# Two attention blocks on one core: units halved by queries, eight-head projections, wider DMA transposes, and maxima as bf16 trees

## The chip, the cores and the metric

The kernel runs on one core of one Trainium2 chip. The metric is the device time of one execution in microseconds (us). A core has TensorE (PE in the profile; PEld is its weight load), VectorE (DVE), ScalarE (ACT), GpSimd (POOL) and SyncE (SP), which here only issues transfers. Each engine works through its own list of instructions in order and waits on semaphores for the others.

## The reference

Two independent blocks, A and B, each over 2048 rows of 512 features, with 32 heads of 16 dimensions. Their outputs stand side by side in the result.

```
# A: softmax attention
q, k, v = split((x @ wqkv).reshape(B, S, 3, H, Dh))
p = softmax(einsum("bhqd,bhkd->bhqk", q, k) * Dh ** -0.5, axis=-1)
a = einsum("bhqk,bhkd->bhqd", p, v).reshape(B, S, D) @ wo
# B: linear attention with a learned feature map
pq, pk = q @ w_phi[h], k @ w_phi[h]
phi(p) = concatenate([softmax(p), softmax(-p)])
kv = phi_k.T @ v;  z = phi_k.sum(rows)
b = (phi_q @ kv / (phi_q @ z + 1e-6)).reshape(B, S, D) @ wo
```

A does nearly all of the work: 32 heads with 2048 x 2048 scores each. B's feature map needs, for each row and head, the maximum and the minimum of 16 values.

## The kernel before

**Units.** A is cut into 32 units: 8 groups `g` of four heads times 4 chunks `c` of 512 queries. The four heads of a group lie on four row groups of TensorE (32 rows each: 16 dimensions, two rows for the maximum, the rest unused), so that matmuls on different row groups run side by side.

**Pass 1** finds the maximum of each query's scores. A unit has 32 steps: a step (`emit_m1`, L889) multiplies 128 queries of two heads with 512 keys into two PSUM banks, and VectorE takes the maximum over the keys (`emit_r1`, L903: 128 partitions x 2 x 512). Two pairs of banks alternate. At the end of a segment (below) `emit_mchain` combines the maxima of the four key chunks (L913), splits their negative into two bf16 parts on POOL (L918 to L921), turns them with a DMA transpose (L923) and writes them into rows of `QT` with two transfers (L926).

**Pass 2** multiplies 128 keys with 512 queries of one head (`block_go`, L954). The maximum is subtracted by the matmul itself, through the extra rows. ScalarE takes the exponential into a ring of 15 buffers (L960), three PSUM banks alternating. A unit has 64 such blocks. After each four, `pv_go` (L1008) multiplies them with the values, the four heads on four column groups, and adds up in bank 7; a column of ones gives the sum. `emit_xev`, `emit_rec` and `emit_mul` (L1137) divide by it. Pass 2 of a segment may start `LAGX` = 8 step slots after its last maximum.

**Segments.** A unit is one segment, but for the first and the last unit, which are cut into two: heads 0 and 1, then heads 2 and 3. Where a batch has only two heads, L1000 fills the other column groups with zero matmuls.

**Background jobs.** Projections of A (`proj`: four matmuls and a copy for each group of four heads and each chunk, L457 with L433, L465 or L469; for the values L445), the output projection (`oproj_job`, L820), and all of B run as jobs in pieces between the steps. B's feature map (`fm`): projection (L583), copy `pB` (L433), maximum and minimum on VectorE (`red`, L593 and L596), subtraction on POOL (L603, L605), exponential (L611), sums and division on POOL; then L697, L746 and L793 for the two products and the output. The last unit's output projection starts with `emit_acc` (L1152), seven matmuls in a lump for each of four row tiles, and ends in `emit_last`.

**The order.** A loop at the end of the kernel writes TensorE's whole list in advance. It goes by a plan of times (`_Clock`: a step 1.131, a matmul of 512 columns 0.215, an exponential 0.477) and puts in a job piece, a PV batch, a block or a step as they fit. Where the plan sees TensorE idle too long, it puts in fill matmuls on zeros, which hold the clock up: on four column groups (`go_fill`, L1101, 256 columns) or on a free row group beside a block (`row_fill`, L1086, 512 columns). At run time nothing is reordered; each instruction waits for its semaphores.

**The head.** x of A comes in 16 DMA transposes of 512 x 128 on SP (L301, four for each chunk of 512 rows), the weights in three loads of 512 columns (L289). VectorE clears the padded weight buffers (L304, L305) and spreads the heads' columns into them (`pad_copy`, L312). SP loads `B_w_phi` with 32 transfers (L517), and transposes B's weights (L529) and x (L533).

Of the kernel before, what the change touches and what calls it, by code (L numbers as in the profile page):

```python
# [6 lines left out]
ALU = mybir.AluOpType  # L7
# [141 lines left out]
def bass_concat_heads__softmax_full_mha__linear_kernel_hedgehog__prompt_kernel(  # L149
# [12 lines left out]
    SPLIT = {0, NU - 1}  # L162
# [20 lines left out]
    for u in range(NU):  # L183
        segs += [(u, (0, 1)), (u, (2, 3))] if u in SPLIT else [(u, (0, 1, 2, 3))]
# [3 lines left out]
    for v, (u, rows) in enumerate(segs):  # L188
        steps = [(v, rows[i] // 2, qt, kc) for kc in range(NKC) for qt in range(4) for i in range(0, len(rows), 2)]
        if u == 0 and v == 1:  # L190
            order[4:4] = steps[0:4]
            steps = steps[4:]
        order += steps
    steps_of = [[q for q, o in enumerate(order) if o[0] == v] for v in range(NV)]
    seg_end = [qs[-1] + 1 for qs in steps_of]
    of_b = [v for v in range(NV) for _ in range(NKT * len(segs[v][1]))]
    seg_b = [of_b.index(v) for v in range(NV)]
    LAG = seg_end[0] + LAGX

    with contextlib.ExitStack() as es:  # L200
# [33 lines left out]
        WQp = sb("WQp", [128, 4, NG, 128], BF)  # L234
        WKp = sb("WKp", [128, 4, NG, 128], BF)
# [15 lines left out]
        pB = sb("pB", [128, 2, 512], F32)  # L251
# [3 lines left out]
        mB = sb("mB", [128, 2, 2, 32], F32)  # L255
# [32 lines left out]
        def load_w(queue, i):  # L288
            t_wa[i] = P.dma(queue, dsem("wa%d" % i), lambda e: e.dma_start(  # L289
                wA[:, :, i * 512:(i + 1) * 512], wa_v[:, :, i * 512:(i + 1) * 512]))  # L290

        load_w("act", 0)
        load_w("act", 1)
        t_xa = {}
        for c in range(NQC):
            d = "xa%d" % c
            dsem(d)
            if c == 1:
                load_w("sp", 2)
            for ct in range(4):  # L300
                t_xa[c] = P.dma("sp", d, lambda e, ct=ct, c=c: e.dma_start_transpose(  # L301
                    xAT[:, ct, c * 512:(c + 1) * 512], A_x[0][c * 512:(c + 1) * 512, ct * 128:(ct + 1) * 128]))

        t_wq0 = P.op("dve", lambda e: e.memset(wqf.bitcast(U32), 0))  # L304
        t_wk0 = P.op("dve", lambda e: e.memset(wkf.bitcast(U32), 0))  # L305
        t_bias = P.op("dve", lambda e: e.tensor_reduce(
            bias_k[:, :], ident[:].rearrange("p (r x) -> p r x", x=32)[:, :, 16:18], AX.XY, ALU.add), [t_ident])

        def pad_copy(dst, col0, dep0):
            src = wA[:, :, col0:col0 + 512].rearrange("p ct (gr d) -> p ct gr d", d=16)  # L310
            dv = dst[:].rearrange("p ct g (r x) -> p ct (g r) x", x=32)[:, :, :, 0:16]
            return P.op("dve", lambda e: e.tensor_copy(dv, src), [t_wa[col0 // 512], dep0])  # L312
# [8 lines left out]
        t_yd1 = P.op("pool", lambda e: e.memset(Yd[:], 1.0))  # L321
        t_vb1 = P.op("pool", lambda e: e.memset(vB[:], 1.0))
# [37 lines left out]
        def add_job(slot, pieces, fin, by=None, when=None):  # L360
            by = slot + BY if by is None else by
            njobs[0] += 1
            jobs.append((by, slot, njobs[0], pieces, fin, when))

        def next_job(tau):

            return min((j for j in jobs if j[1] <= tau and (j[5] is None or j[5]())), default=None)

        ck = _Clock(12.0)
# [6 lines left out]

        def bg_at(tau):

            if running:
                left = running[0][0]  # L380
                return (ck.full("full", running[0][4]), left[0][0]) if left else None
            j = next_job(tau)
            if j is None or not ring_free:
                return None
            return ck.full("full", min(ring_free)[0]), j[3][0][0]

        def bg_go(tau):
            if not running:
                j = next_job(tau)
                jobs.remove(j)  # L390
                free, bank = ring_take()
                running.append([list(j[3]), j[4], bank, bank_reader.get(bank), free, None, j[0]])
            r = running[0]
# [9 lines left out]
        def bg_read(tau, by):  # L403


            if running and not running[0][0] and running[0][4] <= by:
                r = running.pop()
# [32 lines left out]
        last_proj = {}  # L440

        def proj(kind, a, c):
            if kind == "v":
# [3 lines left out]
                    start=(ct == 0), stop=(ct == 3)), [t_xa[kt // 4], t_wa[2]])  # L447
# [8 lines left out]
            wpad = WQp if kind == "q" else WKp  # L456
            pieces = mm_pieces(lambda e, b, ct: e.matmul(  # L457
                PS[:, b, :], wpad[:, ct, g, :], xAT[:, ct, c * 512:(c + 1) * 512],
                start=(ct == 0), stop=(ct == 3)), [t_xa[c], t_wqp if kind == "q" else t_wkp])

            def fin(b, tok, tau):
                last_proj[kind] = tok
                sl = slice(c * 512, (c + 1) * 512)
                if kind == "q" and g == 0 and c == 0:
                    t = P.op("dve", lambda e: e.tensor_copy(QT[:, g, sl], PS[:, b, :]), [tok])  # L465
                elif kind == "q":
# [4 lines left out]
                (qt_ready if kind == "q" else kt_ready)[(g, c)] = t  # L471
                return t
# [6 lines left out]
        XA = (9.0, 15.0, 19.5, 24.5)  # L479
        need = [(8, "k", 0, 1), (12, "k", 0, 2), (16, "k", 0, 3)]  # L480
# [6 lines left out]
        for g in range(2, NG):  # L487
            for t in group(g):
                add_job(at, *proj(*t), by=at + 10)
                at += 4  # L490
# [835 lines left out]
```

## Time and profile before

| | before |
|---|---|
| time of the runs | 1285.52 us median of 3 (1283.88 to 1287.56) |
| profiled execution: time / span | 1283.74 us / 1282.0 us |
| granted TensorE clock | 0.998 |
| PE, DVE, ACT, POOL busy, share of the span | 95%, 95%, 92%, 47% |
| maxima of pass 1 (L903) | 1024, 1170.2 us |
| exponentials of pass 2 (L960) | 2048, 1062.0 us |
| copies of B's maps: maxima and minima (L593, L596) | 32 each, 21.6 us each |
| maxima chains (L913) | 34, 6.9 us |
| DMA: share of 16 engines, main queue | 13.6% |

Busy times are unions: instructions of one engine that overlap count once. The span runs from the first to the last instruction of the core; the time of a run has some 2 us more. A row of the groups reads: line, engine, operation, result<-operands with shapes, count, then busy us and mean ns of one, then the idle time of the engine just before these instructions and what ended most of it.

### The profile page before, as it was taken

To read this page: it belongs to the slowest core of one execution; us is meant where nothing else is said; L and a number is where in the kernel's file an instruction comes from. 1 tells how busy PE (TensorE), PEld (TensorE's weight loads), DVE (VectorE), ACT (ScalarE), POOL (GpSimd) and SP (SyncE) were. 2 spreads that over 40 slices of the span, in tenths; PEclk is the share of its full clock that TensorE was granted. 3 is DMA by queue.
4 is the path that set the end of the run, shared out by engine and by line. 5 is a ranking of instruction groups with operands and counts; after the bars stand their busy time and mean duration, and the time that the engine had idled before them with its cause. 6 is when DMAs were issued, how large, how long until landed. Compare 5 with 4: busy or idle time off the path is not lost.

```text
span 1282.0 us, 28798 instructions
## 1 busy us (share of the span) xinstructions
PE 1219.7 (95%) x12059; PEld 408.0 (32%) x12059; DVE 1214.9 (95%) x1132; ACT 1180.3 (92%) x2321; POOL 600.8 (47%) x620
## 2 busy tenths in 40 slices
PE   8999999999999999999999999999999999999998
PEld 2223333333332233333333333333333233333333
DVE  8999999999999999999999999999999999999920
ACT  3789999999998999999999899999999999999986
POOL 2000102544655565546646346556555554646640
PEclk9999999999999999999999999999999999999999
DMA  6212200000001000000001110112211202121110
GB/s 132 60 16 40 35 7 4 7 7 7 7 6 19 6 8 7 7 6 3 7 7 7 23 24 11 31 19 20 32 19 27 36 15 32 23 24 19 29 20 21
DMA packets 75209, 26.69 MB, mean 21 GB/s; under 512 B 65928, under 2 KB 73096, under 8 KB 75080
## 3 DMA queue, kind: packets, MB, share of 16 engines
q1 hardware_dynamic: 73736, 23.56, 13.6%
q8 instruction: 94, 1.54, 0.5%
q10 hardware_dynamic: 1344, 1.31, 0.3%
q14 instruction: 35, 0.29, 0.1%
HBM read 3.16 MB, written 4.19 MB: 6 GB/s over the span
## 4 chain that ended last, share of the span: by engine, by line
ACT 51%; PE 27%; DVE 21%; issue 1%; DMA 0%; SPq 0%; ACTq 0%
ACT pT L960 45%; DVE part L903 20%; PE PS L954 7%; PE PS L889 4%; PE PS L457 3%; PE PS L1101 3%; PE PS L1008 2%; PE PS L583 2%; ACT eB L611 1%; PE PS L445 1%; PE PS L793 1%; PE PS L684 1%; ACT X L433 1%; ACT pB L433 1%; PE PS L1152 1%
## 5 line engine op out<-in xcount | busy, mean ns | idle before, releaser
L903 DVE TENSOR_REDUCE part<-PS 128x2 f32<-128x1024 f32 x1024 | 1170.2, 1215 | 5.7 <-PE PS L889 2.2
L960 ACT ACTIVATE pT<-PS 128x512 bf16<-128x512 f32 x2048 | 1062.0, 637 | 67.2 <-PE PS L954 27.0
L954 PE MATMUL PS<-QT,KT 32*128 32x512 bf16 x2048 | 657.1, 384 | 18.1 <-ACT pT L960 2.6
L1086 PE MATMUL PS<-zmv,ones_t 32*128 32x512 bf16 x1745 | 581.9, 382 | 0.3 <-ACT X L433 0.2
L889 PE MATMUL PS<-KT,QT 32*128 32x512 bf16 x2048 | 447.3, 383 | 14.1 <-DVE part L903 10.6
L954 PEld LDWEIGHTS PS<-QT,KT 32*128 32x128 bf16 x2048 | 176.9, 91 | 400.0 <-ACT pT L960 243.7
L1008 PE MATMUL PS<-pT,VP 128*17 128x512 bf16 x2048 | 210.7, 384 | 9.9 <-ACT pT L960 0.8
L918 POOL TENSOR_SCALAR stage<-mrow 128x16 bf16<-128x16 f32 (+1 forms) x34 | 8.8, 259 | 332.9 <-DVE mrow L913 332.9
L1101 PE MATMUL PS<-zmv,ones_t 128*17 128x256 bf16 x3028 | 146.7, 276 | 1.5
L1086 PEld LDWEIGHTS PS<-zmv,ones_t 32*128 32x128 bf16 x1745 | 143.3, 91 | 1.7 <-ACT X L433 1.1
L889 PEld LDWEIGHTS PS<-KT,QT 32*128 32x128 bf16 x2048 | 97.5, 91 | 122.3 <-DVE part L903 90.3
L1122 POOL TENSOR_TENSOR lr<-lr,neg 128x16 f32<-128x16 f32 x31 | 90.1, 2906 | 80.6 <-DMA lr<-X 80.5
L1008 PEld LDWEIGHTS PS<-pT,VP 128*17 128x17 bf16 x2048 | 51.4, 87 | 130.2 <-issue 69.3
L769 POOL TENSOR_TENSOR den_t<-den_t,neg 128x32 f32<-128x32 f32 x16 | 87.1, 5445 | 1.3
L641 POOL TENSOR_TENSOR wB<-wB,neg 128x32 f32<-128x32 f32 x16 | 87.0, 5440 | 0.8
L1101 PEld LDWEIGHTS PS<-zmv,ones_t 128*17 128x17 bf16 x3028 | 60.5, 90 | 80.4 <-issue 70.2
L1137 POOL TENSOR_TENSOR QT<-X,Yd 128x256 bf16<-128x256 f32 x62 | 43.8, 728 | 55.7 <-DMA Yd<-Yd 55.7
L618 POOL TENSOR_TENSOR sB<-eB 128x512 f32<-128x512 bf16 x32 | 36.9, 1154 | 67.3 <-ACT eB L611 67.3
L661 POOL TENSOR_TENSOR wA<-eB,rB 128x512 bf16<-128x512 bf16 x64 | 67.0, 1069 | 1.6
L603 POOL TENSOR_TENSOR uB<-pB,mB 128x512 f32<-128x512 f32 x32 | 33.9, 1060 | 52.0 <-DVE mB L593 52.0
L1176 DVE TENSOR_TENSOR QT<-PS,Yd 128x256 bf16<-128x256 f32 x2 | 0.8, 419 | 52.4 <-ACT Yd L1171 52.4
L583 PE MATMUL PS<-WKp,xBT 128*128 128x512 bf16 x128 | 38.0, 384 | 1.7 <-ACT pT L960 0.2
(85 smaller groups left out, 671.5 us busy)
## 6 DMA issues: line engine op xcount, KB each, us to landing
Yd<-Yd SPq DMA_DIRECT2D x124, 32.0 KB, 3.2
out_dram<-xAT SPq DMA_DIRECT2D x16, 128.0 KB, 1.8
out_dram<-OA SPq DMA_DIRECT2D x12, 128.0 KB, 1.7
wA<-in_A_wqkv_dram ACTq DMA_DIRECT2D x2, 512.0 KB, 5.1
QT<-mcols SPq DMA_DIRECT2D x60, 4.0 KB
mcols<-stage SPq DMA_TRANSPOSE x34, 2.3
wA<-in_A_wqkv_dram SPq DMA_DIRECT2D x1, 512.0 KB, 4.3
WOp<-in_A_wo_dram SPq DMA_DIRECT2D x4, 128.0 KB, 4.2
```

The source lines that it names most:

```text
L583: add_job(slot, mm_pieces(lambda e, b, ct: e.matmul(PS[:, b, :], xBT[:, ct, st * 128:(st + 1) * 128], Wf[:, x, ct, :], start=(ct == 0), st ...
L641: t = P.op("pool", lambda e: e.tensor_tensor(wB[:, n % 4, :], wB[:, n % 4, :], neg1[:, 0:1].broadcast_to([128, 32]), ALU.pow), [cx["r"], t ...
L661: t = P.op("pool", lambda e, a=a: e.tensor_tensor(f4[:, :, a, :], e4[:, :, a, :], r2[:, :, 1 - a].unsqueeze(2).broadcast_to([128, H, 16]), ...
L769: cx["rd"] = P.op("pool", lambda e: e.tensor_tensor(den_t[:, :], den_t[:, :], neg1[:, 0:1].broadcast_to([128, 32]), ALU.pow), [t, t_neg])
L889: tok = P.op("pe", lambda e, r=r, bank=2 * (q1 % 2) + i: e.matmul(PS[:, bank, :], QT[32 * r:32 * r + 32, g, q0:q0 + 128], KT[32 * r:32 * r ...
L903: r1[q1] = P.op("dve", lambda e: e.tensor_reduce(part[:, u % 2, 2 * pr:2 * pr + 2, qt, kc], PS[:, b:b + 2, :], AX.X, ALU.max), deps)
L954: m2_t[B] = P.op("pe", lambda e: e.matmul(PS[:, bank, :], KT[32 * r:32 * r + 32, g, kt * 128:(kt + 1) * 128], QT[32 * r:32 * r + 32, g, c ...
L960: exp_t[B] = P.op("act", lambda e: e.activation(pT[:, slot, :], PS[:, bank, :], ACT.Exp, scale=0.25), [m2_t[B], slot_reader.get(slot)])
L1008: tok = P.op("pe", lambda e, B=B, r=r: e.matmul(PVB[32 * r:32 * r + 17, :], VP[:, kt, 4 * g + r, :], pT[:, B % RING, :], start=(kt == 0), ...
L1086: fill_tok[0] = P.op("pe", lambda e: e.matmul(PS[:, 7, :], ones_t[32 * r:32 * r + 32, :], zmv[32 * r:32 * r + 32, :], start=False, stop=Fa ...
L1101: P.op("pe", lambda e, cq=cq: e.matmul(PS[32 * cq:32 * cq + 17, bank, 0:256], ones_t[:, 0:17], zmv[:, 0:256], start=(bank != 7), stop=(ban ...
L1122: rec = P.op("pool", lambda e: e.tensor_tensor(lr[:, ub, :], lr[:, ub, :], neg1[:, 0:1].broadcast_to([128, 16]), ALU.pow), [lr_t[u], t_neg])
```

## The change

It has five parts.

1. **Segments are runs of queries, not pairs of heads.** Every unit is cut into two segments of 256 queries, with all four heads; the first unit into 128, 128 and 256, the last into 256, 128 and 128. A block of pass 2 still fills a bank of 512 columns: with 256 queries it holds two key tiles (`per` = 2, two matmuls of 256 columns on the same row group), with 128 queries four. PV batches follow, eight matmuls of 256 columns for four of 512. The zero fills L1000 go. The key matrix has its heads' dimensions in even rows and ones in odd rows, so the maximum's two parts go to rows 1 and 17 of each group and one transfer writes them.
2. **Eight-head projections.** For groups 2 to 7, a projection of q or k makes 128 columns, eight heads at once. ScalarE copies it to a staging tile, and two transfers of 64 partitions x 512 spread it to the rows of the two groups. POOL presets these rows. Groups 0 and 1 keep the padded way.
3. **Wider DMA transposes.** x of A and B: one transpose of 512 x 512 for each chunk, instead of four; B's weights in 4 instead of 8; `B_w_phi` in 8 transfers instead of 32. A's weights come in five loads, the columns of the first two groups first.
4. **B's maxima and minima** of two maps at a time, as two trees of pairwise bf16 maxima and minima, interleaved; `pB` and `mB` become bf16.
5. **The plan.** It starts at 8.5 instead of 12.0, knows when projections are ready (`m1_from`), can have two jobs in hand, and runs `emit_acc`'s matmuls as a job in pieces.

```diff
-    SPLIT = {0, NU - 1}
+    SPLIT = {**{u: (2, 2) for u in range(NU)}, 0: (1, 1, 2), NU - 1: (2, 1, 1)}
@@ order
-    for v, (u, rows) in enumerate(segs):
-        steps = [(v, rows[i] // 2, qt, kc) for kc in range(NKC) for qt in range(4) for i in range(0, len(rows), 2)]
+    for v, (u, q0, nq) in enumerate(segs):
+        steps = [(v, pr, qt, kc) for kc in range(NKC) for qt in range(q0, q0 + nq) for pr in range(2)]
         if u == 0 and v == 1:
-            order[4:4] = steps[0:4]
-            steps = steps[4:]
+            order[2:2] = steps[0:2]
+            steps = steps[2:]
@@ head
-            if c == 1:
-                load_w("sp", 2)
-            for ct in range(4):
-                t_xa[c] = P.dma("sp", d, lambda e, ct=ct, c=c: e.dma_start_transpose(
-                    xAT[:, ct, c * 512:(c + 1) * 512], A_x[0][c * 512:(c + 1) * 512, ct * 128:(ct + 1) * 128]))
+            t_xa[c] = P.dma("sp", dsem("xa%d" % c), lambda e, c=c: e.dma_start_transpose(
+                xAT[:, :, c * 512:(c + 1) * 512], A_x[0][c * 512:(c + 1) * 512, :]))
+            if c == 2:
+                load_w("sp", 1024, 1536)
+        load_w("sp", 128, 512)
+        load_w("sp", 640, 1024)
@@ eight-head projections
+        def rows_of(g):
+            t_kt1[g] = P.op("pool", lambda e: e.memset(KT[:, g:g + 2, :].bitcast(U32), 0x3F803F80))
+            t_qt0[g] = P.op("pool", lambda e: e.memset(QT[:, g:g + 2, :].bitcast(U32), 0))
...
+                if g >= 2:
+                    i = n_oct[0] % 2
+                    n_oct[0] += 1
+                    t = aevac(oct_t[:, i, :], PS[:, b, :], [tok, oct_d.get(i)])
+                    dst, dep = (QT, t_qt0) if kind == "q" else (KT, t_kt1)
+                    for gg in range(2):
+                        oct_d[i] = P.dma("sp", d_oct[i], lambda e, gg=gg: e.dma_start(
+                            dst[0:128:2, g + gg, sl], oct_t[64 * gg:64 * gg + 64, i, :]), [t, dep[g]])
...
-        for g in range(2, NG):
+        for g in range(2, NG, 2):
             for t in group(g):
                 add_job(at, *proj(*t), by=at + 10)
-                at += 4
+                at += 6
@@ red
-                cx["mx"] = P.op("dve", lambda e: e.tensor_reduce(mB[:, i, 0, :], p3, AX.X, ALU.max),
-                                [cx["p"]] + use(("m", i)))
-                ck.extra += 1.19
-                cx["mn"] = P.op("dve", lambda e: e.tensor_reduce(mB[:, i, 1, :], p3, AX.X, ALU.min), [cx["p"]])
+                if i == 0:
+                    first_map[:] = [cx, sub]
+                    return
+                ops = (ALU.max, ALU.min)
+                src = pB[:].rearrange("p a (h f) -> p (a h) f", f=16)
+                t3 = [uB[:, 0, 256 * k:256 * k + 256].bitcast(BF).rearrange("p (h f) -> p h f", f=8) for k in range(2)]
+                ts = [P.op("dve", lambda e, k=k: e.tensor_tensor(t3[k], src[:, :, 0:8], src[:, :, 8:16], ops[k]),
+                           [cx["p"], first_map[0]["p"]] + use(("u", 0))) for k in range(2)]
+                for w in (4, 2):
+                    ts = [P.op("dve", lambda e, k=k, w=w: e.tensor_tensor(
+                        t3[k][:, :, 0:w], t3[k][:, :, 0:w], t3[k][:, :, w:2 * w], ops[k]), [ts[k]]) for k in range(2)]
+                ts = [P.op("dve", lambda e, k=k: e.tensor_tensor(
+                    mB[:, :, k, :].unsqueeze(3), t3[k][:, :, 0:1].rearrange("p (a h) f -> p a h f", a=2),
+                    t3[k][:, :, 1:2].rearrange("p (a h) f -> p a h f", a=2), ops[k]),
+                    [ts[k]] + use(("m", 0)) + use(("m", 1))) for k in range(2)]
+                ck.extra += 1.85
@@ emit_mchain
-            for hl in range(2):
-                mr_t[v] = P.dma("sp", d_mr[vb], lambda e, hl=hl: e.dma_start(
-                    QT[32 * rows[0] + 16 + hl:32 * rows[-1] + 32:32, g, c * 512:(c + 1) * 512],
-                    mcols[n * hl:n * hl + n, vb, :]), [mt_t[v]])
+            mr_t[v] = P.dma("sp", d_mr[vb], lambda e: e.dma_start(
+                QT[1:128:16, g, c * 512 + qs * 128:c * 512 + (qs + nq) * 128], mcols[0:2 * n, vb, :]), [mt_t[v]])
@@ block_go
-            m2_t[B] = P.op("pe", lambda e: e.matmul(
-                PS[:, bank, :], KT[32 * r:32 * r + 32, g, kt * 128:(kt + 1) * 128],
-                QT[32 * r:32 * r + 32, g, c * 512:(c + 1) * 512],
-                start=True, stop=True, tile_position=(32 * r, 0)),
-                [bank_reader.get(bank), mr_t[v], kt_ready[(g, kt // 4)]])
+            lo, w = c * 512 + qs * 128, nq * 128
+            for j in range(per):
+                m2_t[B] = P.op("pe", lambda e, j=j: e.matmul(
+                    PS[:, bank, j * w:j * w + w], KT[32 * r:32 * r + 32, g, (kt + j) * 128:(kt + j + 1) * 128],
+                    QT[32 * r:32 * r + 32, g, lo:lo + w],
+                    start=True, stop=True, tile_position=(32 * r, 0)),
+                    [bank_reader.get(bank), mr_t[v], kt_ready[(g, kt // 4)]] if j == 0 else [],
+                    signal=(j == per - 1))
@@ pv_go
+            for j in range(per):
+                for B in Bs:
+                    r = blk[B]
+                    tok = P.op("pe", lambda e, B=B, r=r, j=j: e.matmul(
+                        PVB[32 * r:32 * r + 17, lo:lo + w], VP[:, kt + j, 4 * g + r, :],
+                        pT[:, B % RING, j * w:j * w + w],
+                        start=(first and j == 0), stop=(kt + j == NKT - 1), tile_position=(0, 32 * r),
+                        skip_group_check=True),
+                        deps, signal=(B == Bs[-1] and j == per - 1))
+                    deps = []
```

## The prediction, made before the changed kernel ran

> **What bounds the kernel now.** I read the page from the top: span, engines, then the groups of instructions.
>
> ```profile
> span 1282.0 us, 28798 instructions
> PE 1219.7 (95%) x12059; PEld 408.0 (32%) x12059; DVE 1214.9 (95%) x1132; ACT 1180.3 (92%) x2321; POOL 600.8 (47%) x620
> ...
> L903 DVE TENSOR_REDUCE part<-PS 128x2 f32<-128x1024 f32 x1024 | 1170.2, 1215 | 5.7 <-PE PS L889 2.2
> L960 ACT ACTIVATE pT<-PS 128x512 bf16<-128x512 f32 x2048 | 1062.0, 637 | 67.2 <-PE PS L954 27.0
> L954 PE MATMUL PS<-QT,KT 32*128 32x512 bf16 x2048 | 657.1, 384 | 18.1 <-ACT pT L960 2.6
> L1086 PE MATMUL PS<-zmv,ones_t 32*128 32x512 bf16 x1745 | 581.9, 382 | 0.3 <-ACT X L433 0.2
> ```
>
> The 1024 maxima of pass 1 (L903) take 1170 of 1282 us and stood idle for 5.7 us in all: VectorE sets the pace. The profiled execution took 1283.74 us, 1.7 more than its span; the median of the runs is 1285.52. My sum is made on the span, and 3.5 us are added at the end.
>
> Next, the timeline of VectorE and that of ScalarE for the last 90 us (columns: start, duration, what; in brackets the idle time before and who ended it).
>
> ```profile
> 1206.99 17.17 DVE L903 TENSOR_REDUCE part<-PS 128x2 f32<-128x1024 f32 x15
> 1224.19 0.18 DVE L913 TENSOR_REDUCE mrow<-part 128x8 f32<-128x32 f32 x1
> 1276.73 0.76 DVE L1176 TENSOR_TENSOR QT<-PS,Yd 128x256 bf16<-128x256 f32 x2 [52.35 <-ACT Yd L1171]
> ```
>
> ```profile
> 1198.69 3.15 ACT L960 ACTIVATE pT<-PS 128x512 bf16<-128x512 f32 x6 [1.37 <-PE PS L889]
> ...
> 1225.62 5.51 ACT L960 ACTIVATE pT<-PS 128x512 bf16<-128x512 f32 x11
> ...
> 1250.22 1.57 ACT L960 ACTIVATE pT<-PS 128x512 bf16<-128x512 f32 x3 [1.65 <-PE PS L954]
> 1253.66 2.16 ACT L960 ACTIVATE pT<-PS 128x512 bf16<-128x512 f32 x4 [1.87 <-PE PS L954]
> 1258.14 0.60 ACT L960 ACTIVATE pT<-PS 128x512 bf16<-128x512 f32 x1 [2.31 <-PE PS L954]
> ...
> 1274.13 0.60 ACT L960 ACTIVATE pT<-PS 128x512 bf16<-128x512 f32 x1 [0.40 <-PE PS L1086]
> ```
>
> VectorE is done with pass 1 at 1224.4; the span ends 57.6 us later. The L960 rows after 1224.4 add up to 72 exponentials. Why so many: unit 30 may start pass 2 only LAGX = 8 slots after its last maximum, 24 steps or 28 us before VectorE is done, so at about 1196, and ScalarE had run dry just then (idle 1.37 us). From there 128 exponentials remain, and 28 us hold 56 of them. So the kernel is 1224 us of VectorE and a 58 us tail that the size of a unit sets.
>
> Last, TensorE closely, since the change doubles its small matmuls. Its timeline at 602 us and at 608 us:
>
> ```profile
> 602.47 0.39 PE L954 MATMUL PS<-QT,KT 32*128 32x512 bf16 x1
> 602.48 0.38 PE L1086 MATMUL PS<-zmv,ones_t 32*128 32x512 bf16 x1
> ...
> 602.64 0.39 PE L954 MATMUL PS<-QT,KT 32*128 32x512 bf16 x1
> ...
> 602.65 0.42 PE L889 MATMUL PS<-KT,QT 32*128 32x512 bf16 x2
> 602.70 0.37 PE L1086 MATMUL PS<-zmv,ones_t 32*128 32x512 bf16 x1
> ```
>
> ```profile
> 608.78 0.40 PE L1101 MATMUL PS<-zmv,ones_t 128*17 128x256 bf16 x8
> ```
>
> Matmuls on different row groups start 4 ns apart, but the second of the pair at 602.65 started only at 602.70, 0.22 us after the row fill of 602.48, and the fill behind it waited too: a matmul whose row is taken holds up all that follow. In the second fence four matmuls of 256 columns are followed by four more on the same column groups: by the single records the second four start 0.105 to 0.115 us after the first, with their weights already issued. So two halves of 256 in a row cost what one of 512 does, about 0.215, but the instruction behind them starts 0.107 later.
>
> **The change, part by part.**
>
> *Shorter tail.* The last unit's segments end 16, 8 and 0 steps before VectorE is done; unit 30 is halved too. Say ScalarE is caught up, as at 1198. Then the first half of unit 31 (32 blocks) opens at T-9 us (T: VectorE done; 16-8 steps of 1.14), and 64 blocks remain from there. At 0.49 us each (x11 in 5.5 us) this is 31.4; five other copies add 2.5 (those in the tail rows of ScalarE); stalls on TensorE, 13 us in the tail now, I take as 4, because the idle rows 1236 to 1260 go with row halves that leave two row groups free and with lumps of seven accumulating matmuls (L1152), and both go. End of exponentials: T+29. From the last one to the end now takes 1282.0-1274.1 = 7.9, so T+37 for T+57.6: **-20.6**. Bounds: -33 (last quarter opens at T+8, 16 blocks of 0.49, then 7.9, nothing late), 0 (ScalarE is behind and nothing is won).
>
> *B's maxima.* Two 128x512 reductions (L593, L596: 0.675 each) per map. Successive L903 start 1.131 apart and last 1.215, so 0.08 of each overlaps the next: 0.59 on the path, 2.36 for a pair of maps, 16 pairs. Instead, eight two-operand instructions with 512, 256, 128 and 64 results for each of two trees, 1920 in all. No such instruction is in the trace. Below: 0.29 ns per element (the 128x2048 bf16 copy L312, 0.694, less 0.1 fixed, as the tiny reduction L306) gives 0.56+0.8 = 1.36; above: 1.12 ns (L593 less 0.1) gives 2.15+0.8 = 2.96. It is nearest the middle, two bf16 operands in place of one: 1.85. 16 x (1.85-2.36) = **-8** (-16 to +10).
> The Trainium skill (VectorE: DVE Perf Modes, The perf-mode tier table) lets a bf16 tensor_tensor reach twice the rate and keeps a reduction at the single one; on its figures the pair would come out at about 1.9, an estimate, which changes the sum by under 1 us.
>
> *Twice as many maxima chains.* 66 segments for 34: 32 more L913. One lasts 0.18 to 0.20, but the next L903 starts 0.09 after it (1206.90, 1206.99): **+3**. Three POOL instructions of 0.25 more per unit lie on an engine 47% busy, and SP gets one more transpose (issue 1.1) and one transfer fewer per segment. If the chain came later than its slack (6 us in the head from the reduction at 35.75 to the first L954 at 41.95, where 8 slots give 9.2), L954 would wait at the head of TensorE's queue with the next L889 behind it; no L954 waits for a transfer now.
>
> *Eight-head projections.* 24 projections fewer: 96 matmuls of 0.216 and their mode changes (0.095 each) are 23 us off TensorE; 24 copies of about 0.49 are 12 us off ScalarE. Neither is the pace: **0**, but it is cover for the next item. 48 more transfers of 64 KB on SP: they must land before unit 2 (step 64) and are planned from slot 30; six POOL memsets (1.8, as L319) come at slot 22.
>
> *Head.* The first maximum is at 11.86, 3.1 us after the first projection (8.74), which waited for x. With four fewer transposes ahead of it (issue 5.2 us for four, 1.3 for one of any size in the rows) and 256 KB of weights in place of 1 MB I put x at 6, so the first maximum at 9.1. But the new order wants key chunk 3 at step 8 instead of 16, so at 9.1+8x1.13 = 18.1, and it has to arrive 2.1 earlier (projection, copy, L889). At the 208 GB/s of the window 0 to 12 us it comes at 16 (two chunks, 512 KB of wA, itself: 2.5 each), without a stall; at the 5.2 us a chunk of now at 21.6, with one of 5.6. I take 2 of it: -2.8+2 = **-1** (-3 to +3).
>
> *Queries halved: L954 in two.* Of 1853 L954 records between 100 and 1200 us, 1221 are followed within 0.11 us by another row-tiled matmul (969 times a row fill, 244 times L889, 8 times L954). Each would push what follows by 0.107: 131 us more for TensorE in 1100. There it streams for 783 us, spends 171 on mode changes and is free for 145 (union of columns/2.4 GHz over the records; pauses up to 0.095 between modes counted as change). So cover exists, with 23 us from the projections, but nearly all of it is used. PV groups in halves cost nothing by the fill row. What reaches VectorE: the time from a step's matmuls (modelled end) to its maximum is under 0.10 us in 10% of steps, 0.29 in 25%, 0.53 in the median. Steps of the first 10% pay the push (102 x 0.107 = 11), the next few where two pushes meet pay a rest: **+15** (0 to +130). ScalarE has slack: 95.7% busy between 200 and 1000 us, half of its exponentials starting 0.04 after their matmul.
> The Trainium skill says of this that matmuls stay in program order and only weight loads are pulled ahead (TensorE: Matmul & The Clock Gate, Step-by-step); the pair at 602.65 agrees. The same page, The mechanism, says weights overlap matmuls in flight only on another row group.
>
> Sum: 1282.0-20.6-8+3+0-1+15 = 1270.4, plus 3.5: **1274 us**.
>
> **Rivals.**
> 1. *TensorE becomes the bound: slower.* Its place is every L954 followed by row-tiled work, its price 0.107 us. Per unit (37.9 us at VectorE's pace) TensorE needs 32.9 now (954 of 1100); 4.5 more and 0.7 less make 36.7. If half of its present free 5 us can't be used, because L889 and L954 wait for banks in a fixed order, it needs 39.2, so 1.3 x 32 = 42 us in place of the 15: 1301. It decides from 2.1 us of unusable time per unit (27 us in all). For it: 243.7 us of TensorE's waits are for exponentials. Against: those waits shrink as TensorE runs later.
> 2. *The cover holds wholly.* No push reaches VectorE: 1259; with the lower tail bound, 1250. For it: three quarters of the maxima have 0.29 us in hand.
> 3. *ScalarE is not caught up at the end,* since late L954 eat its slack: tail -9 in place of -20.6, so 1285, about no change.
> 4. *Weights of the second half do not load under the first* (the page's second rule, applied to one row group): 2048 x 0.09 (L954's weight load) = 184 us more on TensorE; with rival 1's terms 45 us per unit, 7.1 x 32 = 227 in place of the 15, so some 1486. The pair at 602.65, whose weights issued while its row was still streaming, speaks against it; 0.02.
>
> **Chances.** My forecast 0.42 (own range 1260 to 1290); rival 1 0.26; rival 2 0.18; rival 3 0.12. A measurement tells apart about 0.3%, 3.9 us. Faster: 0.85 of the first, all of rival 2, a quarter of rival 3: 0.57. Same: 0.10. Slower: rivals 1 and 4 and what is left, 0.33. Range: from 1250 (rival 2 with its tail) to 1312 (rival 1 with 10 us more).
>
> **What would show it.** L903: first start near 9, idle under 25 us, last end near 1222; rival 1 puts its idle at 40 and over, released by L889 at TensorE. After it 35 to 40 us to the end. The trees: eight rows of together 1.6 to 2.2 us a pair. Single records of L954: halves 0.105 to 0.115 apart; 0.2 would be rival 4. I am wrong if VectorE's last maximum ends after 1245, or if the tail stays over 50.

## The result, and the profile after

The changed kernel takes 1302.26 us (median of 4 runs, 1295.11 to 1305.29) against 1284.7 before (the median of four runs, the three above and one more): a ratio of 1.0125, 95% interval 1.0076 to 1.0174. It is slower, where 1274 and faster were forecast. The profiled execution took 1295.11 us, with a span of 1293.4.

The page of the changed kernel, the lines that answer to those shown of before, and the row of the granted clock:

```profile
span 1293.4 us, 38893 instructions
PE 1222.3 (95%) x16990; PEld 487.5 (38%) x16990; DVE 1213.8 (94%) x1229; ACT 1165.0 (90%) x2296; POOL 632.8 (49%) x724
...
PEclk9999999999999799999999989999989999999999
...
L988 DVE TENSOR_REDUCE part<-PS 128x2 f32<-128x1024 f32 x1024 | 1174.8, 1215 | 21.6 <-PE PS L974 9.9
L1048 ACT ACTIVATE pT<-PS 128x512 bf16<-128x512 f32 x2048 | 1055.2, 636 | 75.4 <-PE PS L1041 38.1
```

The row of the clock on the page of before:

```profile
PEclk9999999999999999999999999999999999999999
```

ScalarE has 15 us less to do, where 12 were costed. But the maxima (now L988) stand idle for 21.6 us instead of 5.7, and the clock row, 9 throughout before, has a 7 and two 8s. The four runs line up by their mean granted clock: 1295.11 us at 0.984, 1299.63 at 0.979, 1304.89 at 0.973, 1305.29 at 0.972. That is 8.5 us for each 0.01. Drawn on to the 0.997 that the runs of before show, the line would end near 1284, so an estimate from these four runs is that up to 18 us of the median go with the clock.

The tail, first VectorE's timeline of the changed kernel, then ScalarE's:

```profile
1239.62 0.17 DVE L998 TENSOR_REDUCE mrow<-part 128x4 f32<-128x16 f32 x1
1269.66 0.76 DVE L1283 TENSOR_TENSOR QT<-PS,Yd 128x256 bf16<-128x256 f32 x2 [29.87 <-PE PS L1246]
```

```profile
1271.92 0.60 ACT L458 ACTIVATE eB<-PS 128x512 bf16<-128x512 f32 x1 [0.76 <-DVE eB L1297]
...
1277.64 0.60 ACT L458 ACTIVATE xAT<-PS 128x512 bf16<-128x512 f32 x1 [5.12 <-PE PS L870]
1289.22 0.60 ACT L458 ACTIVATE xAT<-PS 128x512 bf16<-128x512 f32 x1 [10.98 <-PE PS L870]
```

From the end of VectorE's last maximum (1239.6) to the end of the copy of A's last output tile (1272.5) it is 33 us, and 44 exponentials are left when VectorE is done; the same count gives 73 before. The shorter tail is there, as forecast. But then two lone copies follow, `xAT` at L458: the last two output tiles of B. In ScalarE's timeline of before, the copy of B's last tile (`xAT`) came 20 us ahead of A's (`eB`):

```profile
1258.63 0.59 ACT L433 ACTIVATE xAT<-PS 128x512 bf16<-128x512 f32 x1
...
1279.06 0.60 ACT L433 ACTIVATE eB<-PS 128x512 bf16<-128x512 f32 x1 [0.75 <-DVE eB L1190]
```

B's last output left at 1259 then, some 22 us before the end; now it leaves at 1290, and A's last two have landed by 1276. What was won at the end of A is hidden behind B.

The lateness of B shows on GpSimd, which takes a long power for each output tile of B, to divide by its sums. Before, one such power (L769) was left after VectorE's last maximum; in the changed kernel there are three (L846). The first row is of before:

```profile
1226.23 5.44 POOL L769 TENSOR_TENSOR den_t<-den_t,neg 128x32 f32<-128x32 f32 x1
```

```profile
1248.02 5.44 POOL L846 TENSOR_TENSOR den_t<-den_t,neg 128x32 f32<-128x32 f32 x1
...
1256.59 5.44 POOL L846 TENSOR_TENSOR den_t<-den_t,neg 128x32 f32<-128x32 f32 x1
...
1267.48 5.44 POOL L846 TENSOR_TENSOR den_t<-den_t,neg 128x32 f32<-128x32 f32 x1
```

The delay is there already ahead of the powers: the last matmuls of B's second product (L746, now L823) start 0.4 us after VectorE's last maximum before and 26.8 us after it in the changed kernel, when A's last exponential has begun. From that product to B's last output it is 35 us before and 24 now. What put the product so late in TensorE's order is not settled; the slots of B's maps are the same in both kernels.

An account of VectorE from the single records of the profiled runs, in us. A wait is what the distance from a maximum to VectorE's next instruction has over 1.131. With 1023 x 1.131 and the last maximum (1.2) the columns add up to the end, to within rounding.

| run | first maximum | waits to 50 us | waits after | chains | B's maxima | last maximum ends |
|---|---|---|---|---|---|---|
| before | 11.9 | 0.4 | 11.7 | 4.1 | 37.9 | 1224.2 |
| after | 10.2 | 4.1 | 24.4 | 8.7 | 33.9 | 1239.6 |
| e2 (reductions) | 10.0 | 4.1 | 17.8 | 6.1 | 37.9 | 1234.2 |
| e7 (reductions, B earlier, middle whole) | 10.2 | 7.8 | 11.9 | 4.2 | 37.9 | 1230.3 |
| e11 (e7 with trees) | 9.5 | 8.6 | 22.4 | 4.3 | 30.1 | 1233.1 |
| e12 (after, B earlier, more fill) | 9.5 | 8.8 | 15.9 | 6.0 | 31.1 | 1229.5 |

### The profile page after: what moved, and what is told of

Read it like the earlier page. It is cut to its first block, busy times and chain, and to the rows that moved or that the text cites. A ratio compares the mean times of both kernels' runs of the same rounds, so it can differ in the third digit from the quotient of the medians.

```text
span 1293.4 us, 38893 instructions
## 1 busy us (share of the span) xinstructions
PE 1222.3 (95%) x16990; PEld 487.5 (38%) x16990; DVE 1213.8 (94%) x1229; ACT 1165.0 (90%) x2296; POOL 632.8 (49%) x724
## 4 chain that ended last, share of the span: by engine, by line
ACT 51%; PE 29%; DVE 18%; issue 1%; DMA 1%; SPq 1%; POOL 0%; DVEq 0%; ACTq 0%
ACT pT L1048 45%; DVE part L988 16%; PE PS L1041 6%; PE PS L974 4%; PE PS L1193 4%; PE PS L1094 3%; PE PS L1178 2%; PE PS L498 2%; PE PS L643 2%; ACT eB L688 1%; PE PS L485 1%; PE PS L870 1%; PE PS L898 1%; ACT X L458 1%; ACT pB L458 1%
## 5 line engine op out<-in xcount | busy, mean ns | idle before, releaser
L988 DVE TENSOR_REDUCE part<-PS 128x2 f32<-128x1024 f32 x1024 | 1174.8, 1215 | 21.6 <-PE PS L974 9.9
L1041 PE MATMUL PS<-QT,KT 32*128 32x256 bf16 (+1 forms) x4224 | 666.1, 272 | 19.6 <-ACT pT L1048 2.1
L1178 PE MATMUL PS<-zmv,ones_t 32*128 32x512 bf16 x1755 | 595.9, 387 | 0.6 <-ACT X L458 0.4
L974 PE MATMUL PS<-KT,QT 32*128 32x512 bf16 x2048 | 452.1, 388 | 17.3 <-DVE part L988 11.8
L1041 PEld LDWEIGHTS PS<-QT,KT 32*128 32x128 bf16 x4224 | 226.5, 92 | 369.7 <-ACT pT L1048 222.9
L1004 POOL TENSOR_SCALAR stage<-mrow 128x8 bf16<-128x8 f32 (+1 forms) x66 | 15.8, 239 | 466.6 <-DVE mrow L998 466.6
L1094 PE MATMUL PS<-pT,VP 128*17 128x256 bf16 (+1 forms) x4224 | 205.5, 275 | 14.0 <-ACT pT L1048 4.8
L1193 PE MATMUL PS<-zmv,ones_t 128*17 128x256 bf16 x3640 | 169.0, 279 | 2.5 <-ACT X L458 2.0
L974 PEld LDWEIGHTS PS<-KT,QT 32*128 32x128 bf16 x2048 | 118.4, 91 | 110.3 <-DVE part L988 74.8
L1178 PEld LDWEIGHTS PS<-zmv,ones_t 32*128 32x128 bf16 x1755 | 144.2, 91 | 3.0 <-PE PS L1178 1.2
L1193 PEld LDWEIGHTS PS<-zmv,ones_t 128*17 128x17 bf16 x3640 | 73.5, 90 | 88.6 <-issue 77.7
L1214 POOL TENSOR_TENSOR lr<-lr,neg 128x16 f32<-128x16 f32 x31 | 90.6, 2922 | 16.9 <-DMA lr<-X 16.9
L846 POOL TENSOR_TENSOR den_t<-den_t,neg 128x32 f32<-128x32 f32 x16 | 87.5, 5467 | 1.3
L1229 POOL TENSOR_TENSOR QT<-X,Yd 128x256 bf16<-128x256 f32 x62 | 44.0, 731 | 66.8 <-DMA Yd<-Yd 66.8
L738 POOL TENSOR_TENSOR wA<-eB,rB 128x512 bf16<-128x512 bf16 x64 | 66.9, 1069 | 0.6
L680 POOL TENSOR_TENSOR uB<-pB,mB 128x512 f32<-128x512 bf16 x32 | 33.5, 1047 | 27.4 <-DVE mB L665 27.4
L698 POOL TENSOR_TENSOR sB<-sB 128x256 f32<-128x256 f32 x64 | 36.1, 564 | 5.0
```

What stands on the lines that cost most here:

```text
L738: t = P.op("pool", lambda e, a=a: e.tensor_tensor(f4[:, :, a, :], e4[:, :, a, :], r2[:, :, 1 - a].unsqueeze(2).broadcast_to([128, H, 16]), ...
L846: cx["rd"] = P.op("pool", lambda e: e.tensor_tensor(den_t[:, :], den_t[:, :], neg1[:, 0:1].broadcast_to([128, 32]), ALU.pow), [t, t_neg])
L974: tok = P.op("pe", lambda e, r=r, bank=2 * (q1 % 2) + i: e.matmul(PS[:, bank, :], QT[32 * r:32 * r + 32, g, q0:q0 + 128], KT[32 * r:32 * r ...
L988: r1[q1] = P.op("dve", lambda e: e.tensor_reduce(part[:, u % 2, 2 * pr:2 * pr + 2, qt, kc], PS[:, b:b + 2, :], AX.X, ALU.max), deps)
L1041: m2_t[B] = P.op("pe", lambda e, j=j: e.matmul(PS[:, bank, j * w:j * w + w], KT[32 * r:32 * r + 32, g, (kt + j) * 128:(kt + j + 1) * 128], ...
L1094: tok = P.op("pe", lambda e, B=B, r=r, j=j: e.matmul(PVB[32 * r:32 * r + 17, lo:lo + w], VP[:, kt + j, 4 * g + r, :], pT[:, B % RING, j * ...
```

## Where the clock goes

The window table of before and of the changed kernel for 400 to 600 us (columns: stretch, length, then busy time and instructions of PE, PEld, DVE, ACT, POOL, then the clock, DMA share and GB/s):

```profile
400.00:600.00 200.00, 190.36 (x1875) 62.67 (x1875) 199.74 (x188) 187.79 (x366) 110.24 (x114) 1.00 0.08 9
```

```profile
400.00:600.00 200.00, 190.67 (x2487) 72.16 (x2489) 194.03 (x197) 184.52 (x364) 112.23 (x122) 0.95 0.09 11
```

The trace's clock records put this 0.95 in one stretch of 20.5 us at half clock, from 434 us on. Here is what preceded it: GpSimd, VectorE and TensorE of the changed kernel, from three timelines.

```profile
427.40 4.33 POOL L738 TENSOR_TENSOR wA<-eB,rB 128x512 bf16<-128x512 bf16 x4
```

```profile
429.81 2.20 DVE L660 TENSOR_TENSOR uB<-pB 128x512 bf16<-128x512 bf16 x2
431.94 0.88 DVE L663 TENSOR_TENSOR uB<-uB 128x256 bf16<-128x256 bf16 x4
432.73 0.44 DVE L665 TENSOR_TENSOR mB<-uB 128x64 bf16<-128x64 bf16 x2
433.09 3.48 DVE L988 TENSOR_REDUCE part<-PS 128x2 f32<-128x1024 f32 x3
```

```profile
432.42 0.64 PE L1041 MATMUL PS<-QT,KT 32*128 32x256 bf16 x3
434.36 0.61 PE L974 MATMUL PS<-KT,QT 32*128 32x512 bf16 x2 [1.31 <-DVE part L988]
```

The two first steps of the trees (L660) took 2.20 us while GpSimd multiplied two of its four tiles (L738). Elsewhere they take 0.75:

```profile
312.20 0.75 DVE L660 TENSOR_TENSOR uB<-pB 128x512 bf16<-128x512 bf16 x2
```

So VectorE took no maximum for 3.3 us, the next step's matmuls (L974) had no free bank, and TensorE stood for 1.31 us. Weighted by the share of the array that streams, TensorE was at work for 32% of the 3.41 us that end at 434.0, and half in the median window. (The windows are counted back from the start of the stretch; a matmul on 32 of 128 rows, or with 17 columns of weights, counts a quarter.) Of such windows the trace of before has one, at 1192 us (32%), and behind it its only stretch before the end; in the changed kernel one of 31 to 33% stands before each of the four stretches (41 us together), and none of 36% or more is followed by one. The same count over all fourteen profiles, from 30 to 1200 us, has 4723 windows at full clock and 21 stretches: each of the 14 windows at 34% or less is followed by half clock, none above 38% is, and between 35 and 38% it goes either way.
The Trainium skill (TensorE: Matmul & The Clock Gate, What's actually happening) has a free-running window of 3413 ns and a half clock after an idle one. The length agrees (20.48 us is six of them); a window a third busy was enough here, which the page doesn't say.

Trees that GpSimd stretches are one cause of such windows, not the only one. In the four profiles with trees and the plan's old fill thresholds (after, e1, e3, e11) 13 pairs of maps keep VectorE for over 2.3 us, and half clock sets in within 8 us behind 8 of them; in the two with more fill (e6, e12) behind none of 5. In the changed kernel the stretches at 434 and 755 us come so, those at 847 and 963 us have no stretched tree near them; shortly before the last, ScalarE stood 2.9 us for a product of GpSimd (L853).

The stretching of trees by GpSimd, over all 32 first tree steps of the changed kernel: 15 that meet nothing on GpSimd last 0.41 to 0.42 us; eight that meet the long powers (L1214, L846) 0.41 to 0.47; the two that meet the products L738 last 0.99 and 1.29, one that meets L798 0.99, and three that meet L1229 0.42 to 0.94. The three left, beside a chain's L1004 or the sum L794, last 0.41 to 0.42. The reductions of e2, with a single input, last 0.675 in the mean, as before the change.
The Trainium skill (SBUF — State Buffer, SBUF: two separate sides) says that a VectorE instruction with two SBUF inputs and a GpSimd instruction that reads SBUF lock one port pair from each other for their whole length. That fits 1.29 as a wait of up to one product (1.07) and 0.415 of its own. By the same rule the powers, which read SBUF too, would hold a tree step up; the eight at 0.41 to 0.47 show no such wait, so there the measurement differs from the page.

## The experiments

Runs and medians in us, ratios to the kernel before with 95% intervals; clock is the span of mean granted clocks over the runs. For e1 it leaves out the profiled execution, 1306.78 us at 0.953.

| run | median | ratio | clock |
|---|---|---|---|
| after | 1302.26 | 1.0125 [1.0076, 1.0174] | 0.972 to 0.984 |
| e1 | 1286.12 | 0.9999 [0.9987, 1.0012] | 0.975 to 0.981 |
| e2 | 1286.91 | 1.0013 [0.9995, 1.0032] | 0.986 to 1.000 |
| e3 | 1294.14 | 1.0072 [1.0053, 1.0090] | 0.984 to 0.991 |
| e4 | 1293.38 | 1.0071 [1.0038, 1.0104] | 0.976 to 0.990 |
| e5 | 1277.57 | 0.9947 [0.9928, 0.9965] | 0.981 to 0.997 |
| e6 | 1297.19 | 1.0097 [1.0079, 1.0115] | 0.993 to 0.997 |
| e7 | 1273.82 | 0.9916 [0.9900, 0.9932] | 0.996 to 0.999 |
| e8 | 1273.93 | 0.9917 [0.9900, 0.9934] | 0.994 to 0.996 |
| e9 | 1276.96 | 0.9937 [0.9914, 0.9959] | 0.992 to 0.998 |
| e10 | 1283.58 | 0.9991 [0.9976, 1.0006] | 0.988 to 0.999 |
| e11 | 1279.66 | 0.9950 [0.9932, 0.9967] | 0.985 to 0.993 |
| e12 | 1277.05 | 0.9941 [0.9924, 0.9957] | 0.995 to 0.997 |

**e1: B's maps earlier.**

```diff
-    FMSTEP = 26
+    FMSTEP = 25
```

> B's 32 maps 25 slots apart instead of 26, so its last map comes 31 slots (35 us) earlier; nothing else changes. Theory (three causes add up: B's last output tiles end 20 us after A's, half-clock stretches cost 14 to 20 us, the halves' push the rest): A's output ends last, span some 16 to 20 us shorter, 1278 to 1288 us, half-clock stretches still there (granted clock 0.97 to 0.99). Rival (the late end of B is an effect of ScalarE and GpSimd being late, not of the slots): B still ends last and the time stays above 1295.

1286.12, 16 us less than the changed kernel, with the clock as low as there. B's end was a loss by itself, of the size expected. That A now ends last is not shown: the one profile is that of the run at 0.953, and there B's last output still lands 0.7 us after A's. In that profile five of the six stretched trees are followed by half clock, the longest pair of maps keeping VectorE for 4.65 us.

**e2: reductions in place of the trees.** `red` is that of before, on the bf16 tiles.

```diff
...
+                cx["mx"] = P.op("dve", lambda e: e.tensor_reduce(mB[:, i, 0, :], p3, AX.X, ALU.max),
+                                [cx["p"]] + use(("m", i)))
+                ck.extra += 1.19
+                cx["mn"] = P.op("dve", lambda e: e.tensor_reduce(mB[:, i, 1, :], p3, AX.X, ALU.min), [cx["p"]])
...
```

> The two trees go back to two tensor reductions per map (on bf16), each map on its own; the halves stay. Theory: no tree can be stretched by GpSimd, VectorE's longest pause in pass 1 falls from 3.3 to 1.2 us, granted clock at 0.99 or more, and B's last two maps do not come as a pair, so B ends earlier: 1262 to 1276 us. Rival (the halves of 256 columns alone starve TensorE's clock and VectorE): clock stays at 0.97 to 0.985 and VectorE's idle before the maxima near 20 us; only B's end gains, 1285 to 1295 us.

1286.91, 15 us less than the changed kernel. The clock came back in most runs, as the theory said and the rival didn't; in the profiles VectorE is done 5.4 us earlier and B 12. The time is above the theory's 1262 to 1276 since B still ends last: its last output leaves at 1278.2, A's at 1267.6. That the maps came in pairs was only part of B's delay. B still ends some 9 us later against VectorE's end than before the change; the last matmuls of its second product start 21.4 us after that end, for 26.8 in the changed kernel and 0.4 before, and what holds them there is not settled.

**e3 and e4: whole units in the middle,** with trees (e3) and with reductions (e4).

```diff
-    SPLIT = {**{u: (2, 2) for u in range(NU)}, 0: (1, 1, 2), NU - 1: (2, 1, 1)}
+    SPLIT = {0: (1, 1, 2), NU - 1: (2, 1, 1)}
```

> The 30 units in the middle go back to one segment of 512 queries; first and last unit stay cut into 128, 128 and 256; trees and all else stay. Theory (trees and B's end are to blame): half-clock stretches remain where trees meet GpSimd, VectorE's idle stays above 12 us, B still ends last: 1288 to 1300 us. Rival (the halves): idle before the maxima falls to 6 us, clock to 0.995, VectorE done at about 1222; B's end alone holds it at 1278 to 1286 us.

> Both undone: whole units in the middle and two reductions per map. Both theories: clock 0.995 or more, VectorE done at about 1225, A's end 35 to 45 us later, B not last: 1262 to 1272 us. If it is no better than e2, the halves cost nothing; if e3 and e2 are both near 1290, each is a cause of its own.

e3 is 8 us faster than the changed kernel, within the theory's range, with the clock at 0.984 to 0.991 and B last (its last output leaves at 1289.1). e4 missed both theories' range. VectorE's timeline of e4 shows why:

```profile
1243.38 0.17 DVE L982 TENSOR_REDUCE mrow<-part 128x4 f32<-128x16 f32 x1
1288.31 0.76 DVE L1267 TENSOR_TENSOR QT<-PS,Yd 128x256 bf16<-128x256 f32 x2 [44.76 <-PE PS L1230]
```

44.8 us between the last chain and the last division, for 29.9 in the changed kernel: 71 exponentials are left when VectorE is done, about as many as before the change (73). So halves in the last unit alone don't shorten what is left. And 27 us of this profile's main part ran at half clock without any tree: other waits do it as well, and the plan leaves little margin.

**e5 to e8.** e5 is e1 and e2 together. e6 is the changed kernel with `COLD` 8.0 and `WARM` 8.4, nothing else. e7 is e5 with only the ends cut. e8 is e5 with `COLD` 7.3 and `WARM` 7.7.

```diff
-    SPLIT = {**{u: (2, 2) for u in range(NU)}, 0: (1, 1, 2), NU - 1: (2, 1, 1)}
+    SPLIT = {0: (1, 1, 2), NU - 2: (2, 2), NU - 1: (2, 1, 1)}
```

> Halves kept; B back to two reductions per map (as e2) and B's maps 25 slots apart (as e1). Theory (the late end of B and the trees' clock stretches are the loss, the halves themselves cost VectorE some 6 us of waits and 2 us of chains): A ends last, 10 us before e2's end: 1270 to 1279 us, clock 0.99 or more, faster than before by about 1%. Rival (e1 and e2 both landed at 1286 because something else holds the end there): 1283 to 1288.

> The changed kernel with the plan's two thresholds for fill matmuls up by one (COLD 8.0 for 7.0, WARM 8.4 for 7.4), nothing else. Theory (half-clock stretches cost about a third of their length, and follow windows of 3.41 us with little work on TensorE): clock 0.99 or more, time 1285 to 1291, B's end still last. Rival (the stretches are only a sign of stalls, or fills get in the way): 1298 to 1306.

> As e5, but only the last two units and the first are cut; units 1 to 29 are whole again. Theory (what halving is worth is won at unit 30 alone; in the middle it only costs pushes and chains): 4 to 10 us faster than e5, 1262 to 1272 us, some 45 exponentials left when VectorE is done. Rival (halves in the middle keep ScalarE caught up, and whole units lose it, as e4's 71 left): 60 or more left, 1278 to 1292 us.

> As e5, with the two fill thresholds up by 0.3 (7.3 and 7.7). Theory: 0 to 4 us faster than e5, with the clock at 0.997 or more in every run. Rival (fills cost as much as they save): same as e5 or slower.

e5: 1277.57, within the theory's range, though the clock of one run fell to 0.981. The two repairs together are worth 25 us, less than the 16 and 15 that each was worth alone. e6: the clock was restored, VectorE done 10 us earlier (1229.8), yet the time fell by 5 only, above the theory's range: 91 exponentials are left at VectorE's end for 44, the last one ends at 1286.5 for 1266.6, and A, not B as expected, ends last. With more fill the exponentials come later, so both theories had a part; whether the fills take the time on the chip or push the blocks back in the list is not shown. Its window row shows what they do restore:

```profile
400.00:600.00 200.00, 189.51 (x2769) 77.83 (x2787) 199.79 (x206) 185.75 (x360) 116.80 (x132) 1.00 0.10 12
```

VectorE is back at 199.8 of 200 us with halves and trees both in place. None of the trees in this stretch met a product of GpSimd, as two did in the changed kernel, so the row shows clock and undisturbed trees together, not the clock alone. e7 and e8: 1273.82 and 1273.93, the fastest of the study, 0.8% under the kernel before. e7 beats e5 by 3.8 us, just short of the 4 to 10 expected and above the theory's 1272, with 63 exponentials left rather than 45 or 71. So halving the middle units has a use (18 exponentials) and a price: waits of 11.9 for about 16 to 18, chains of 4.2 for 6. (In e5's own profile the waits are 21.7, with 10 us of half clock in the main part.) Use and price are about even: e8, with the middle halved, is 3.6 us faster than e5 and level with e7. Its clock of 0.994 to 0.996 fell short of the 0.997 expected.

**e9, e10: the head.** e9 is e7 with 22 warm-up matmuls, the number before the change, which had cut them to 11; e10 adds `COLD` 7.5 and `WARM` 7.9.

```diff
-        for i in range(11):
+        for i in range(22):
```

> As e7, with 22 warm-up matmuls at the start again instead of 11. Theory (the pause of TensorE after 11 of them puts the clock at half from 12 to 22 us, and the maxima of the head wait 8 us instead of 4 for it): no half-clock stretch in the head, waits of the head 3 to 5 us, 2 to 4 us faster than e7. Rival (the head waits for x and the weights, not for the clock): waits unchanged at 7 to 8 us, time as e7.

> As e9, with the fill thresholds at 7.5 and 7.9. Theory: clock 0.997 or more in every run, 0 to 3 us faster than e9: 1267 to 1272. Rival (e6: fills take the exponentials' place): slower than e9 by 2 to 6 us.

e9: the head's waits fell from 7.8 to 4.8, as expected, and its half clock from 10.2 us to 3.4. But the first maximum came at 12.2 instead of 10.2, and the time is not shorter: 3 us longer in the median, with intervals that overlap. e10: 6.6 us slower still, a little past the rival's 2 to 6, with 75 exponentials left: the rival, fills in the exponentials' way.

**e11: the trees by themselves,** e7 with the trees in place of the reductions.

> As e7 (two last units halved, B 25 slots apart), with the trees in place of the reductions: the trees by themselves. Theory (a tree costs 1.80 us a pair where GpSimd is quiet or takes a power, up to 3.3 where it multiplies, and can starve TensorE into a half-clock stretch): VectorE spends 31 to 35 us on B instead of 37.9, but some runs have stretches; median within 4 us of e7, spread of the runs wider. Rival (the trees are a plain gain of 8 us, as forecast): 1265 or less. Second rival (the trees alone carry the loss): 1282 or more.

1279.66, 5.8 us slower than e7 and more spread; a little past the 4 us expected. In the profile, of the slowest of its six runs, VectorE spends 7.8 us less on B, what the prediction had costed, and loses it again in waits: 22.4 for 11.9, with 27 us of half clock in the main part. One tree step of 1.28 us met the product L853, and a stretch of 10 us follows it; the other stretch, of 17 us, has no stretched tree before it.

**e12: all five parts kept, only the plan's numbers changed** (`FMSTEP` 25, `COLD` 7.6, `WARM` 8.0).

> All five parts of the change kept, trees and halves too; only the plan's numbers differ: B's maps 25 slots apart, fill thresholds 7.6 and 8.0. Theory (the loss is B's late end, 16 us, and the half-clock stretches, some 9 to 14 us; the parts themselves are sound): clock 0.99 or more, 1272 to 1282 us. Rival (the trees and halves cost what no clock gives back): 1284 or more.

1277.05, 25 us below the changed kernel and 0.6% under before: within the theory's range. It differs from e1 by the fill alone, which is worth 9 us there, where B's end is no longer in the way. The change's parts can stay; what made it slower is where B ended and how close the plan ran TensorE to the clock's limit. That each part earns something is not shown: e7, without trees and with the middle units whole, is 3 us faster than e12.

## Why the prediction was wrong, point by point

**Two terms were missing.** The tail's T+37 was taken for the end of the kernel, and B's end was put at nothing: its last output left at 1259 in the trace of before, and I did not ask what comes last when A's tail shrinks by 20 us. It is worth 16 us (e1). And the clock, at 0.998 before, was taken as given, though the account used the very idle time of TensorE that the fills are there for. More fill gave 5 us back in e6, behind B's late end, and 9 between e1 and e12; the line through the four runs puts the clock at up to 18. The sum 1274 misses the 1302 by 28; the two together gave back 25 (e12).

**Tail of A: right.** T+37 was forecast; A's last copy starts at T+32 and its outputs land some 3 us later. The condition, that ScalarE is caught up, takes halves in the middle units too: with whole ones 71 exponentials are left (e4), with only unit 30 halved as well 63 (e7), with all of them halved 44.

**B's maxima: right size, wrong price.** Undisturbed, a pair of maps takes 1.81 us (at 312.20), forecast 1.85. But four of 16 pairs took 2.8 to 3.3, each beside a product or sum of two tiles on GpSimd: 33.9 us in all for 37.9, -4 and not -8. Such a pause can be followed by half clock, which the sum did not have.

**Chains: +3 forecast, +4.6 measured** (e2: +2). **Projections: 0 forecast;** no run takes this part out, so it is not shown by itself. **Head: -1 forecast, +2.0 measured:** the first maximum is 1.7 earlier, not 2.8, and 3.7 more of waits follow. In e7's timeline of SP the three first transposes of 512 x 512 take 7.55 us to issue, 1.4 to 3.7 each, where I had taken one issue to cost 1.3 at any size.

**Halved queries: the reading fell.** I had read the pair at 602.65 as proof that a matmul whose row is taken holds up all behind it, and priced 1221 pushes from it. The changed kernel's timeline says otherwise:

```profile
430.72 0.28 PE L1041 MATMUL PS<-QT,KT 32*128 32x256 bf16 x1
...
430.73 0.38 PE L1178 MATMUL PS<-zmv,ones_t 32*128 32x512 bf16 x1
...
430.84 0.27 PE L1041 MATMUL PS<-QT,KT 32*128 32x256 bf16 x1
```

`block_go` writes the two halves (L1041) one behind the other, and the row fill (L1178) after them; on the chip the fill started between them. In 1323 of 1984 pairs one to three fills or matmuls of pass 1 start between the halves, which lie 0.120 us apart in the median. So the push that I priced isn't there. The rows at 602 don't contradict it: the second L889 starts 0.227 us after the L954 of 602.47, and the fill behind it 0.226 us after the fill of 602.48, so each can have waited for its own row alone. What the halves cost VectorE is the 4 to 6 us of waits between e7 and e8, e12 or e2 (10 to e5, with its half clock), whose mechanism stays open; the +15 was too high, and 12.7 in the profile is that and the half clock. The rule that matmuls stay in program order, which I quoted from the Trainium skill (TensorE: Matmul & The Clock Gate, Step-by-step), does not hold across row groups here, and neither does what I wrote of the order, that nothing is reordered at run time.

**The rivals.** Rival 1 (TensorE bound, 1301) hit the number by chance: its mechanism was the push. TensorE, free of half-clock stretches, keeps pace (e6). Rival 2 had the mechanism nearest to what the records show, no push, but its 1259 lacks the same two terms. (Its lower end should be 1247: 12.4 less than 1259, not 9.) Rival 3 was not seen (44 exponentials left: ScalarE was caught up). Rival 4 is refuted by the 0.120. No rival was B's end or the clock, though the prediction's own check would have led there: it called itself wrong if the tail stays over 50 us, and it is 53.8, of which the last 18 are B's.

## What to carry to other kernels

When the path at the end gets shorter, look up who ended second, and by how little. Where an engine's idle time is filled on purpose to hold a clock, every new pause of a neighbour has to be weighed against that margin, and more fill is not free either. An instruction with two inputs that is cheap alone is to be costed beside what GpSimd runs at that moment.

## What the runs showed of the hardware

- TensorE's matmuls on different row groups do overtake one that waits for its own row: 1323 of 1984 pairs.
- One 3.41 us window with TensorE a third busy or less was followed by half clock: all 14 at 34% or less in the fourteen profiles, none above 38%. Stretches lasted 3.4 to 20.5 us in the profiles of before and after, up to 61 us in e1's. Over the changed kernel's four runs 0.01 of mean clock went with 8.5 us.
- A two-input bf16 instruction of VectorE, 0.415 us alone, took up to 1.29 us beside a GpSimd product; beside GpSimd's long powers it took 0.41 to 0.47, and a one-input reduction of the same tile 0.675 throughout.
- A DMA transpose of 512 x 512 took 1.4 to 3.7 us to issue, one of 512 x 128 1.2 to 1.3 at the same place in the head.
